# Softmax sums by halves of the queries instead of odd and even key steps, in an attention kernel with a feed-forward layer

## The chip, the cores and the metric

The kernel runs on one core of one Trainium2 chip. The metric is the device time of one execution in microseconds (us). The kernel before takes 433.28 us, the median of six runs from 433.18 to 434.18.

## What is computed

Eight batches, twelve heads, 448 positions, head size 64. Queries and keys are normalised by their root mean square and scaled by a gain, then softmax attention, then a feed-forward layer with a leaky ReLU over the 12 x 64 = 768 features of each of the 3584 positions:

```python
def _attn_ref(q, k, v, g_q, g_k):
    q_n, k_n = (rmsnorm(q, g_q), rmsnorm(k, g_k))
    scores = scale * np.matmul(q_n, k_n.transpose(0, 1, 3, 2))
    scores = scores - np.max(scores, axis=-1, keepdims=True)
    attn = np.exp(scores)
    attn = attn / (np.sum(attn, axis=-1, keepdims=True) + 1e-09)
    return np.matmul(attn, v).astype(np.float32)
...
    h = x @ w_in                       # 3584x768 by 768x2048
    g = np.maximum(0.01 * h, h)
    return (g @ w_out).astype(np.float32)   # 2048x768
```

The division by the sum of the exponentials is what the change touches.

## The kernel before

**Units.** Four heads of one batch are a unit; there are 24, three to a batch. The four heads are numbered by r and a (0 or 1 each). A unit's 448 keys are worked in seven key steps of 64; with r on the two halves of the partitions a step is a tile of 128 rows (2 x 64 keys), and a picks one of two column blocks of 448 queries. The scores stand transposed, keys on partitions and queries in columns, so that the exponentials `et` (128 x 7 steps x 2 x 448, fp16) are at once the moving operand of the product with V.

**Order.** Everything is issued in an order written out by hand (`manual_schedule`). From unit 3 on, a loop goes through units u and four stages d of each. Stage 0 makes the score step 0 of unit u (`qk`, L182), its column maximum on VectorE (`shift_max`, L219 and the diagonal `dg`, L221), the product with V of unit u - 1 (`pv_slot`, L326), the sums of u - 1 (`zcol`, L269), the matmul that spreads the maximum of u (`shift_mm`, L231), from which VectorE takes the shift `eb` (L232, L240), a copy of the product to SBUF on ScalarE (`pv_out`, L281), the addition of the two half sums on VectorE (`zcol_sum`, L286 and L287), and then the exponentials of u (`ex`, L201). The first job after that is `zcol_inv`: the reciprocal as Ln and Exp on ScalarE (L291, L292), and DMAs on SyncE's queue (SP) that spread the reciprocals `zs` over the partitions of `rz` (L296). Behind them on that queue stand the loads of q and k for unit u + 4 (L108) and the stores of results. In stage 1 GpSimd (POOL) multiplies the copied product by `rz` into `xt` (`xmul_pool`, L306), for u from 5 to 7 VectorE does that in stage 2. Stage 2 also has the normalisation of unit u + 2: `rinv` on ScalarE (L147, L148), `n` on VectorE (L154) and its transpose by DMA (L166). Stage 3 squares the rows for unit u + 3 on ScalarE (L131).

**Filling.** Between the attention work of each stage `fill` puts items of the feed-forward layer of earlier batches, by their costs: the first matrix in `moe1` (`hps`, L347, and the leaky ReLU `gt`, L341, on ScalarE), the second in `moe2` (`op`, L387) or in `seven`, which needs seven products where the plain form needs eight (`ma`, `mb`, `mc`, `md`, L427) and prepares sums of operands `sa` and adds results to `ost` on VectorE (L408 to L417, L434).

**The sums.** This path is used for units 4 to 22, 19 in all (`narrow`). A weight of 128 x 32 ones and zeros, `onesr`, adds over the 64 keys of each r, so one matmul gives the sums of two heads on 32 partitions. Four such column tiles of TensorE, at partitions 32 x (2y + a) of the bank `zc`, work side by side. Before, y is the parity of the key step: steps 0, 2, 4 go to y = 0, steps 1, 3, 5 to y = 1, each over all 448 queries, and step 6 is split, its first 224 queries to y = 0 and the others to y = 1. The sum of a query is then the sum of the two rows, which is formed by a copy of 64 x 448 and an addition:

```python
        s["zs"] = zpool.tile([64, S], FP32, tag="zs", name="zs")
        nc.vector.tensor_copy(s["zs"], s["zc"][64:128, 0:S])
        nc.vector.tensor_tensor(s["zs"], s["zc"][0:64, 0:S], s["zs"], op=ALU.add)
```

Row 32a + 2i + r of `zs` holds the sums of head (r, a) sixteen times over, and each of the two DMAs reads 32 rows of 1792 bytes, four times each, into all 128 partitions.

Of the kernel before, what the change touches and what calls it, by code (L numbers as in the profile page):

```python
# [8 lines left out]
FP32 = mybir.dt.float32  # L9
FP16 = mybir.dt.float16  # L10
AF = mybir.ActivationFunctionType
ALU = mybir.AluOpType
AXL = mybir.AxisListType
# [5 lines left out]
def kernel(  # L19
# [11 lines left out]
    nc = tc.nc  # L31

    B, H, S, D = q.shape
    QH = 4
    NS = 7
    P = 128
# [13 lines left out]
    zpool = ctx.enter_context(tc.tile_pool(name="zpool", bufs=1))  # L50
# [4 lines left out]
    def aux(shape, dtype, name):  # L55
        return psum.tile(shape, dtype, tag="aux", bufs=4, name=name)
# [5 lines left out]
    onesr = cst.tile([P, 32], FP16)  # L62
# [184 lines left out]
    def zsum(u, t0=0, t1=NS):  # L247
        s = st[u]
        for t in range(t0, t1):
            for r in range(2):  # L250
                for a in range(2):
                    nc.tensor.matmul(s["zt"][r][64 * a:64 * a + 64, 0:S], ones16[64 * r:64 * r + 64],
                                     s["et"][64 * r:64 * r + 64, t, a], start=(t == 0), stop=(t == NS - 1))

    def zsum_slot(u):
# [2 lines left out]
        s["zt"] = [s["zslot"][:, r] for r in range(2)]  # L258
        zsum(u)

    def zcol(u):
        s = st[u]
        s["zc"] = aux([P, 512], FP32, "zc")
        for t in (0, 1, 6, 2, 3, 4, 5):
            for a in range(2):
                halves = ((t % 2, 0, S),) if t < NS - 1 else ((0, 0, S // 2), (1, S // 2, S))
                for y, lo, hi in halves:
                    c = 32 * (2 * y + a)
                    nc.tensor.matmul(s["zc"][c:c + 32, lo:hi], onesr, s["et"][:, t, a, lo:hi],  # L269
                                     start=(t < 2), stop=(t in (4, 5)))  # L270

    def pv_slot(u):
        s = st[u]
# [8 lines left out]

    def zcol_sum(u):
        s = st[u]
        s["zs"] = zpool.tile([64, S], FP32, tag="zs", name="zs")
        nc.vector.tensor_copy(s["zs"], s["zc"][64:128, 0:S])  # L286
        nc.vector.tensor_tensor(s["zs"], s["zc"][0:64, 0:S], s["zs"], op=ALU.add)  # L287

    def zcol_inv(u):
        s = st[u]  # L290
        nc.scalar.activation(s["zs"], s["zs"], AF.Ln)  # L291
        nc.scalar.activation(s["zs"], s["zs"], AF.Exp, bias=0.0, scale=-1.0)  # L292
        s["rz"] = zpool.tile([P, 2, S], FP32, tag="rz", name="rz")
        for r in range(2):
            src = s["zs"][r:64:2, None, :]
            nc.sync.dma_start(s["rz"][:, r], src.broadcast_to([32, 4, S]))  # L296

    def xmul_sb(u):
        xmul_pool(u, nc.vector)
# [276 lines left out]
    with tc.manual_schedule():  # L576
# [171 lines left out]
        for u in range(3, NU):  # L748
            for d in range(4):
                if d > 0 or u > 3:  # L750
                    qk(u, STEPS[d])
                    if d == 0:
                        shift_max(u)
                        if narrow(u - 1):
                            pv_slot(u - 1)
                            zcol(u - 1)
                            shift_mm(u)
                            pv_out(u - 1)
                            zcol_sum(u - 1)
                        else:  # L760
                            zsum_slot(u - 1)
                            pv(u - 1)
                            shift_mm(u)
                            zinv(u - 1)
                    ex(u)
# [5 lines left out]
                if d == 0:  # L771
                    if u == 3:
                        prep_norm(4)
                        gate(4)
                    elif narrow(u - 1):
                        job(zcol_inv, u - 1)
                    else:
                        xmul(u - 1)
                    if u + 4 < NU:
                        job(load, u + 4)  # L780
                    if u + 3 < NU:
                        load_v(u + 3)
                    if u < 6:
                        prep_sqp(u + 3)
# [63 lines left out]
```

The softmax here doesn't subtract the row's maximum and nothing guards it: scores larger than these inputs give would overflow.

## Time and profile before

| What | Value |
|---|---|
| median of six runs | 433.28 us |
| the profiled execution's own time | 433.18 us |
| its span (first to last instruction) | 431.4 us |
| granted TensorE clock, mean | 0.99 |
| DMA traffic | 62.37 MB, 145 GB/s on average |
| first and last reduction of zs (L286) begin at | 78.9 and 369.1 us |
| zc matmuls (L269) | 304: 16 in each of 19 units |
| rz DMAs (L296) | 38, 224 KB each, 2.9 to 3.7 us from issue to landing |

PE is TensorE's matmuls, PEld its weight loads, DVE VectorE, ACT ScalarE, POOL GpSimd, SP the queue of SyncE. A row of a group gives line, engine, operation, output and inputs, count, and times in nanoseconds (least, median, most). In the timeline the first two columns are start and length in us, and the bracket gives how long the engine stood idle before the instruction and what ended that. In the table of waits come total us, number of times, and the longest. Times of single instructions in the text are starts in us from the beginning of the span. The share of busy time of PE is not its share of peak, since matmuls are pipelined.

### The profile page before, as it was taken

Reading aid. Unit: us, or ns where it says so; the run is one execution under the profiler, and the core shown is the slowest. Engines: PE = TensorE matmul, PEld = TensorE weight load, DVE = VectorE, ACT = ScalarE, POOL = GpSimd, SP = SyncE. Lnnn points to the kernel's source line nnn. Section 1 sums busy time; section 2 is a strip of 40 time slices with the busy share of each in tenths; the row PEclk is TensorE's granted clock in tenths of the full one; section 3 lists DMA queues with packets and bytes.
Section 4 is the critical chain, followed back from the end, with each engine's and each line's share of the span. In section 5 each row is a group of like instructions: output and inputs, shape, how many; then the busy total and the mean of one; then the engine's idle time right before and its main releaser. Section 6 shows DMA issues by size and latency. Waiting matters only on the chain.

```text
span 431.4 us, 8844 instructions
## 1 busy us (share of the span) xinstructions
PE 409.5 (95%) x3645; PEld 211.0 (49%) x3645; DVE 273.4 (63%) x434; ACT 306.1 (71%) x466; POOL 86.7 (20%) x77
## 2 busy tenths in 40 slices
PE   7677999999989999999999999999999999999996
PEld 6444444445444544454445544454445544455563
DVE  5898656888568865487369864587359840542162
ACT  4389888757986779966986789966986757643400
POOL 3875323300002102112102102111101101010000
PEclk9699999999999999999999999999999999999999
DMA  7999993789557896568655897478572460212013
GB/s 254 196 241 250 238 251 99 132 176 235 146 100 118 189 206 164 145 125 212 159 100 139 171 207 169 133 139 207 150 109 45 118 142 17 44 38 73 2 44 103
DMA packets 66476, 62.37 MB, mean 145 GB/s; under 512 B 35716, under 2 KB 61572, under 8 KB 66436
## 3 DMA queue, kind: packets, MB, share of 16 engines
q1 hardware_dynamic: 55840, 49.62, 46.7%
q0 software_dynamic: 10272, 11.80, 17.4%
q8 instruction: 28, 0.46, 0.4%
q10 hardware_dynamic: 324, 0.39, 0.3%
q14 instruction: 12, 0.10, 0.1%
HBM read 45.61 MB, written 11.01 MB: 131 GB/s over the span
## 4 chain that ended last, share of the span: by engine, by line
PE 62%; ACT 16%; DVE 13%; issue 4%; DMA 1%; SPq 0%; ACTq 0%; DVEq 0%
PE hps L347 25%; ACT et L201 8%; PE ma L427 7%; PE md L427 6%; PE sT L182 5%; PE sT L326 4%; PE mc L427 4%; DVE n L154 4%; PE op L387 3%; PE mb L427 3%; ACT gt L341 3%; PE zc L269 2%; DVE sT L219 1%; DVE ssq L142 1%; PE sT L231 1%
## 5 line engine op out<-in xcount | busy, mean ns | idle before, releaser
L201 ACT ACTIVATE et<-sT,eb 128x896 f16<-128x896 f32 x166 | 158.3, 1004 | 15.7 <-PE sT L182 13.3
L347 PE MATMUL hps<-xt,win 128*128 128x448 f16 x756 | 151.0, 353 | 0.2 <-DVE xt L335 0.2
L347 PEld LDWEIGHTS <-win 128*128 128x128 f16 x756 | 70.6, 98 | 71.4 <-issue 9.9
L341 ACT ACTIVATE gt<-hps 128x448 f16<-128x448 f32 x126 | 65.6, 540 | 20.2 <-PE hps L347 19.5
L306 POOL TENSOR_TENSOR xt<-x,rz 128x896 f16<-128x896 f32 x16 | 33.4, 2090 | 150.5 <-DMA rz<-zs 49.7
L154 DVE TENSOR_TENSOR n<-rq,rinv 128x896 f16<-128x896 f32 (+2 forms) x25 | 29.0, 1163 | 48.1 <-ACT rinv L148 44.6
L182 PE MATMUL sT<-qkT 64*64 64x448 f16 x664 | 52.7, 367 | 4.8 <-ACT et L201 4.4
L142 DVE TENSOR_REDUCE ssq<-sq 128x14 f32<-128x896 f32 (+2 forms) x49 | 50.1, 1054 | 1.4 <-ACT sq L131 1.4
L427 PEld LDWEIGHTS <-sa 128*128 128x128 f16 x352 | 32.8, 98 | 26.3 <-issue 6.1
L281 ACT COPY x<-sT 128x896 f32<-128x896 f32 x19 | 17.2, 905 | 39.5 <-DVE sT L232 39.5
L111 POOL DMA_DIRECT2D vt<-in_v_dram x24 | 18.2, 758 | 114.6 <-PE sT L326 107.1
L427 PEld LDWEIGHTS <-gt 128*128 128x128 f16 x264 | 25.2, 98 | 20.3 <-issue 4.3
L219 DVE TENSOR_REDUCE sT<-sT 128x1 f32<-128x896 f32 x22 | 24.0, 1091 | 17.4 <-PE sT L182 17.4
L182 PEld LDWEIGHTS <-qkT 64*64 64x64 f16 x672 | 15.8, 104 | 39.0 <-issue 36.0
L387 PE MATMUL op<-wout,gt 128*128 128x384 f16 x192 | 34.1, 327 | 0.0
L427 PE MATMUL ma<-wout,gt 128*128 128x384 f16 x176 | 32.3, 326 | 0.1
L154 DVE TENSOR_TENSOR n<-rk,rinv 128x896 f16<-128x896 f32 (+2 forms) x25 | 28.9, 1156 | 0.0
L326 PE MATMUL sT<-et,vt 64*64 64x448 f16 x532 | 28.5, 349 | 0.3
L408 DVE TENSOR_TENSOR sa<-gt 128x512 f16<-128x512 f16 (+1 forms) x15 | 8.1, 542 | 29.5 <-ACT gt L341 29.5
L326 PEld LDWEIGHTS <-vt 64*64 64x64 f16 x672 | 20.4, 107 | 10.9 <-issue 1.1
L387 PEld LDWEIGHTS <-gt 128*128 128x128 f16 x192 | 17.7, 98 | 14.0 <-issue 3.2
L453 ACT COPY ost<-ma 128x384 f32<-128x384 f32 x11 | 5.3, 478 | 23.6 <-PE ma L427 23.6
(87 smaller groups left out, 444.5 us busy)
## 6 DMA issues: line engine op xcount, KB each, us to landing
rq<-in_q_dram SPq DMA_DIRECT2D x24, 448.0 KB, 4.8
rk<-in_k_dram SPq DMA_DIRECT2D x24, 448.0 KB, 6.0
out_dram<-ost SPq DMA_DIRECT2D x52, 192.0 KB, 3.9
rz<-zs SPq DMA_DIRECT2D x38, 224.0 KB, 3.3
vt<-in_v_dram POOLq DMA_DIRECT2D x24, 224.0 KB, 5.0
win<-in_moe_w_in_dram POOLq DMA_DIRECT2D x8, 384.0 KB, 9.1
wout<-in_moe_w_out_dram POOLq DMA_DIRECT2D x2, 1536.0 KB, 23.6
out_dram<-ost SPq DMA_DIRECT2D x4, 96.0 KB, 2.1
```

The costliest lines, as they stand in the source:

```text
L111: nc.gpsimd.dma_start(vts[u % NV].rearrange("p a t d -> p a (t d)"), rows(v, u))
L142: nc.vector.tensor_reduce(buf(u, "ssq")[:, ti, :, c[0]:c[1]], buf(u, f"sq{ti}")[:, :, c[0]:c[1]], axis=AXL.X, op=ALU.add)
L154: nc.vector.tensor_tensor(buf(u, "n16")[:, ti, c[0]:c[1]].rearrange("p s a d -> p a s d"), src[:, :, c[0]:c[1]], buf(u, "rinv")[:, ti, :, ...
L182: nc.tensor.matmul(banks[a][64 * r:64 * r + 64, 0:S].rearrange("p (t x) -> p t x", t=NS), kT(u, r, a, t), qT(u, r, a), start=True, stop=True)
L201: nc.scalar.activation(s["et"][:, t], sT[:, :, 0:S], AF.Exp, bias=s["eb"], scale=1.0)
L219: nc.vector.tensor_reduce(s["spare"][:, 511:512], sT[:, :, 0:S], axis=AXL.XY, op=ALU.max)
L306: eng.tensor_tensor(xts[b][:, g], s["x32"], s["rz"], op=ALU.mult)
L326: nc.tensor.matmul(s["pv"][r][64 * a:64 * a + 64, 0:S], vts[u % NV][64 * r:64 * r + 64, a, t], s["et"][64 * r:64 * r + 64, t, a], start=(t ...
L341: nc.scalar.activation(dst, src, AF.Prelu, bias=0.0, scale=1.0, alpha=0.01)
L347: nc.tensor.matmul(hps[:, 0:S], win16[:, kt // 2, kt % 2, ts(ft, P)], xt[:, kt // 2, kt % 2], start=(kt == 0), stop=(kt == KT - 1))
L387: nc.tensor.matmul(op2[:, 0:HC], gt[:, ft, ds(col(t), P)], wout16[:, ft, ds(HC * half, HC)], start=(ft == 0), stop=(ft == FT - 1))
L427: nc.tensor.matmul(bank[:, 0:HC], a[:, f], b[:, f], start=(first and f == 0), stop=(f == HF - 1), skip_group_check=not first)
```

## The change

The column tiles y now stand for the halves of the queries, not for the parity of the steps: tile y takes queries 224y to 224y + 223 of all seven steps. One matmul takes two key steps, as two runs of 224 columns side by side in the bank (steps 0 and 1, 2 and 3, 4 and 5), and step 6 alone fills the first 224 columns only. Each of the 128 partitions then has two columns for a query, 224 apart, and one VectorE reduce adds them. `zs` is 128 x 224 in place of 64 x 448, so are Ln and Exp, and four DMAs of half the size spread it, since a head's sums lie on two groups of partitions. The order of the instructions on every engine is otherwise as before.

```diff
+    HS = S // 2
+
     def zcol(u):
         s = st[u]
         s["zc"] = aux([P, 512], FP32, "zc")
-        for t in (0, 1, 6, 2, 3, 4, 5):
-            for a in range(2):
-                halves = ((t % 2, 0, S),) if t < NS - 1 else ((0, 0, S // 2), (1, S // 2, S))
-                for y, lo, hi in halves:
+        for i, (t, n) in enumerate(((0, 2), (NS - 1, 1), (2, 2), (4, 2))):
+            for y in range(2):
+                for a in range(2):
                     c = 32 * (2 * y + a)
-                    nc.tensor.matmul(s["zc"][c:c + 32, lo:hi], onesr, s["et"][:, t, a, lo:hi],
-                                     start=(t < 2), stop=(t in (4, 5)))
+                    nc.tensor.matmul(s["zc"][c:c + 32, 0:n * HS].rearrange("p (k x) -> p k x", k=n), onesr,
+                                     s["et"][:, t:t + n, a, HS * y:HS * y + HS], start=(i == 0), stop=(i == 3))
...
     def zcol_sum(u):
         s = st[u]
-        s["zs"] = zpool.tile([64, S], FP32, tag="zs", name="zs")
-        nc.vector.tensor_copy(s["zs"], s["zc"][64:128, 0:S])
-        nc.vector.tensor_tensor(s["zs"], s["zc"][0:64, 0:S], s["zs"], op=ALU.add)
+        s["zs"] = zpool.tile([P, HS], FP32, tag="zs", name="zs")
+        nc.vector.tensor_reduce(s["zs"], s["zc"][:, 0:S].rearrange("p (k x) -> p x k", k=2), axis=AXL.X, op=ALU.add)
...
     def zcol_inv(u):
...
         for r in range(2):
-            src = s["zs"][r:64:2, None, :]
-            nc.sync.dma_start(s["rz"][:, r], src.broadcast_to([32, 4, S]))
+            for y in range(2):
+                src = s["zs"][64 * y + r:64 * y + 64:2, None, :]
+                nc.sync.dma_start(s["rz"][:, r, HS * y:HS * y + HS], src.broadcast_to([32, 4, HS]))
```

## The prediction

> **What bounds the kernel now.** I read the head of the page and its slices first, then the tables of waits, then the timeline around each wait of TensorE (PE), and last the tiles zs, zc and rz, which the change touches.
>
> ```profile
> span 431.4 us, 8844 instructions
> ...
> PE 409.5 (95%) x3645; PEld 211.0 (49%) x3645; DVE 273.4 (63%) x434; ACT 306.1 (71%) x466; POOL 86.7 (20%) x77
> ...
> PE   7677999999989999999999999999999999999996
> ```
>
> From slice 8 on PE is full. An engine that gets less to do brings nothing by that alone; only what shortens a wait of PE counts. The table of waits has these for PE after the first units:
>
> ```profile
> PE sT L182 <- ACT et L201: 4.4, 11, 0.9
> ...
> PE sT L231 <- DVE dg L221: 2.3, 4, 1.1
> ...
> PE md L427 <- DVE ost L434: 1.3, 4, 0.3
> ```
>
> L231 is the shift's matmul, which waits for the diagonal dg; its four waits stand in the timeline at 91.64 (0.81), 122.34 (1.10), 185.89 (0.17) and 282.51 us (0.22). Of the 4.4 us at L182 only two, 0.26 us each, lie where the change works (83.41 and 96.94); the others lie before 73 us, ahead of the first zc at 77.21. So all that is to be had is about 4.1 us, and part of it hangs on engines that the change does not help.
>
> **What the change costs and saves by itself.** The rows of tile zs:
>
> ```profile
> L296 SPq DMA_DIRECT2D rz<-zs x38: 520/586/649, 81.6 to 372.9; - x38
> L286 DVE COPY zs<-zc x19: 626/627/628, 78.9 to 369.1; 64x448 f32<-64x448 f32 x19
> L287 DVE TENSOR_TENSOR zs<-zc,zs x19: 616/616/619, 79.5 to 369.8; 64x448 f32<-64x448 f32 x19
> L291 ACT ACTIVATE zs<-zs x19: 566/569/571, 80.4 to 371.1; 64x448 f32<-64x448 f32 x19
> L292 ACT ACTIVATE zs<-zs x19: 576/577/577, 81.0 to 371.7; 64x448 f32<-64x448 f32 x19
> ```
>
> *PE.* 16 zc matmuls a unit before and after; each of the four column tiles streams 3 x 448 + 224 columns either way, four tiles at a time, in the same places of PE's order. The 16 take 0.85 us in the timeline. The moving data now come in two runs of 224; the score matmuls (L182) read seven runs of 64 at 367 ns each against 353 ns for hps, which reads one run. I take 0. Upper end: one round of four (0.19 us between starts) lost in each unit, 19 x 0.19 = 3.6 us. Lower end 0, since no column goes away.
>
> *VectorE.* Copy and add, 0.627 + 0.616 = 1.24 us, become one reduce over 448 PSUM elements a partition. The nearest row is L214, a reduce of 128x448 from PSUM at 0.61 us. Saved 0.63 us a unit, 12 us in all. It buys no time: the next VectorE work after zs at 81 and 94.5 us first waits 0.80 us for PE (op L387), and elsewhere VectorE waits 4 to 6 us for rinv a little later. Should the stride of 224 make it twice as slow, it costs the pair's 1.24 us again and hides as the pair does.
>
> *ScalarE.* Ln and Exp go from 448 to 224 elements a partition. Ln: 128x448 takes 0.534 and 128x896 0.917 (L316, L312), 0.19 for 224, so 0.569 becomes 0.38; with the 128x28 row (0.329, L147) it would be 0.44. Exp: 0.576 and 0.950 (L317, L313), so 0.577 becomes 0.39. Saved 0.32 to 0.38; I take **0.35 us a unit**.
>
> *SyncE and the DMAs.* Two rz transfers become four of half the bytes. Each issue takes 0.586 us, so the last one is issued 1.76 us after the first, not 0.59, and all that SP issues behind it (the loads of q and k, output stores) comes 1.17 - 0.35 = 0.8 us later. The loads are four units ahead; the stores' buffers are four deep, and the transposes of the normalised tile, the next SP work with a deadline, begin 0.85 us (87.98), 1.4 us (101.38) and elsewhere over 2.5 us after the end of such a burst. I charge 0; where that cover were gone, 0.8 us a unit of a transpose that is itself read some 5 us later.
>
> **The one price that decides.** POOL multiplies x by rz (L306) when the last rz has landed, and VectorE's normalisation (L154) does not run beside it:
>
> ```profile
> 178.81 2.07 POOL L306 TENSOR_TENSOR xt<-x,rz 128x896 f16<-128x896 f32 x1 [8.06 <-ACT et L201]
> ...
> 180.30 0.23 ACT L148 ACTIVATE rinv<-uu 128x28 f32<-128x28 f32 x1
> ...
> 180.56 1.28 DVE L154 TENSOR_TENSOR n<-rq,rinv 128x896 f16<-128x896 f32 x1 [5.75 <-ACT rinv L148]
> 181.76 1.08 DVE L154 TENSOR_TENSOR n<-rk,rinv 128x896 f16<-128x896 f32 x1
> ...
> 185.89 0.22 PE L231 MATMUL sT<-dg,onesp 128*128 128x64 f16 x2 [0.17 <-DVE dg L221]
> ```
>
> The first n lasts 1.28 us, not 1.08: its work begins only when POOL ends at 180.88. So when rz lands matters. Call d the landing of the last of four pieces, less that of the last of two, both from the first issue. Now the first piece lands 2.9 us after its issue and the second 3.6 to 3.7 after its own, so 4.2 to 4.3 after the first issue; the two landings lie 1.3 us apart though the issues lie 0.59 apart, so the transfers queue. Half the bytes at half the time (0.65) would end at 2.9 - 0.65 + 3 x 0.65 = 4.2 us: d = 0. A lower end: only the issues limit, 1.76 + 2.25 = 4.0, d = -0.2. An upper end: each piece holds the queue as long as a whole one, 2.9 + 3 x 1.3 = 6.8, d = +2.5. I take **d = 0**: the nearest row is this same transfer, and its queue shows that bytes, not the count, set its pace now. Exp ends 0.35 earlier, so POOL's xt moves by -0.35 + d. Behind xt on POOL stands only the next load of v, which waits for PE's pv anyway (107.1 us in all).
>
> The Trainium skill speaks against splitting: "DMA: Bandwidth & Descriptors", Rules for kernel authors, says of two transfers to disjoint halves that one should not bother, they serialize, and that small ones should be coalesced. Its fit (2.0 us plus bytes over 436 GB/s, for the other kind of queue) gives, as an estimate, 2.3 us for a half piece, so 1.76 + 2.3 = 4.1 us and d = -0.1 to -0.2 if the halves don't serialize, and more if they do. "SBUF — State Buffer", Door 1, says that 64 partitions reach only half of the DMA ports, and the same ones for 0..31 and 0..63; by it, the pieces from the upper 64 partitions use the other half of the ports and queue less, d below 0. No row before the change shows such a piece.
>
> **The sum, wait by wait.**
> - 122.34 us, 1.10: ScalarE is busy 12.77 of 13.00 us from 108 to 121, n at 115.53 had waited 4.09 us for rinv, and from there VectorE runs without a break to dg. The multiply there is VectorE's own, so POOL plays no part. Ln and Exp lie ahead of rinv in this run: **-0.35**.
> - 96.94 us, 0.26: the exponentials at 95.00 come behind Exp, their scores are there from about 94.8: **-0.2**. The same at 83.41 is given back at 91.64, where VectorE is busy from 80.97 on and sets the end.
> - 185.89 and 282.51: rinv and POOL's xt both come 0.35 earlier, VectorE's run to dg too, and the 0.17 + 0.22 go: **-0.4**.
> - 91.64 (0.81) and the four at md (0.31 each): set by VectorE's own run and by PE's scores; 0.
>
> Sum -0.95 us against the profiled execution's own 433.18 us (span 431.4, the rest outside it), which is the lowest of the six runs; their median is 433.28, 0.1 above: **432.2 us**. A measurement of this kernel tells about 0.2%, 0.87 us, from no change.
>
> **Rivals.**
> 1. *Hidden anyway, 432.8 (432.4 to 433.6).* Each of the four waits is followed back through a chain in which PE sets other links (the ost copies wait for op, exponentials for scores). If these end next, half of the 0.95 or nothing is left. For it: PE at 95%; against it: ScalarE without a break before 115.5 and 180.6.
> 2. *Late rz: slower.* Place: POOL's xt ahead of n. In four stages n begins 0.2 us after POOL ends, as here, and PE waits for md behind it:
>
> ```profile
> 147.03 2.07 POOL L306 TENSOR_TENSOR xt<-x,rz 128x896 f16<-128x896 f32 x1 [7.49 <-ACT ost L453]
> ...
> 149.33 1.09 DVE L154 TENSOR_TENSOR n<-rq,rinv 128x896 f16<-128x896 f32 x1 [0.31 <-ACT rinv L148]
> ```
>
> These four lose from d = 0.35 + 0.2 = 0.55 on, the two dg stages from d = 0.35. At d = 1.2 xt is 0.85 late: 4 x 0.65 + 2 x 0.85 = 4.3, less the 0.55 of the first two terms: +3.8, 437. At d = 2.5, 2.15 late: 4 x 1.95 + 2 x 2.15 + some 1.5 in each of two further stages with n behind xt (165.92, 213.41) - 0.55 = 14.6, 448. It decides from d = 0.8, where the loss passes 0.87 us. Against it: bytes halve, and the queue is free between the issues.
> 3. *The matmuls do not keep their rate*, up to +3.6 less 0.95: 436. Nothing in the rows speaks for it but that no zc row reads two runs. The change would then not do what it says, the same work in fewer instructions.
>
> **How the numbers follow.** Forecast 0.43, rival 1 0.36, rival 2 0.16, rival 3 0.05. Faster by over 0.2% is the forecast, 0.43; within it 0.36; slower 0.16 + 0.05 = 0.21. The likeliest case alone is 431.6 to 432.4. The range goes from 431.2 (all waits of ScalarE's making gone, and d = -0.2) to 434.6 (d = 0.9 in rival 2); it leaves out some 0.15 above, most of rivals 2 and 3.
>
> **What would show it.** zc: 16 matmuls in 0.85 us again. zs: one reduce at 0.6 us, Ln and Exp at 0.35 to 0.45. rz: the time from the first issue to POOL's xt (now 147.03 - 142.80 = 4.2 us): 4.2 proves d = 0, above 5 rival 2. The waits of L231 near 122 down to 0.75, near 185 and 282 gone. The prediction is wrong if n still starts where it did (rival 1), or if the waits at md grow above 0.31.

## The result and the profile after

The median after is **432.47 us** (431.50 to 433.13, 19 runs), against 433.54 us for the kernel before in the same comparison (432.46 to 434.87, 41 runs): 1.07 us less, a ratio of 0.9975, 95% interval 0.9968 to 0.9981. The profiled span went from 431.4 to 430.4 us. The diff adds one line, so L296 of before is L297 here, L306 is L307, L427 is L428 and L434 is L435.

The head of the page and its engines, after:

```profile
span 430.4 us, 8910 instructions
...
PE 409.0 (95%) x3645; PEld 210.5 (49%) x3645; DVE 261.8 (61%) x415; ACT 300.6 (70%) x466; POOL 86.4 (20%) x77
```

VectorE is busy for 11.6 us less and ScalarE for 5.5 us less, but the span is only 1.0 us shorter. The rows of tile zs, after (line, engine, operation, tiles, count; least, median and most ns; first and last start):

```profile
L297 SPq DMA_DIRECT2D rz<-zs x76: 520/597/1458, 81.2 to 372.8; - x76
L287 DVE TENSOR_REDUCE zs<-zc x19: 614/625/626, 78.7 to 367.9; 128x224 f32<-128x448 f32 x19
L291 ACT ACTIVATE zs<-zs x19: 389/399/401, 80.3 to 369.9; 128x224 f32<-128x224 f32 x19
L292 ACT ACTIVATE zs<-zs x19: 389/389/391, 80.8 to 370.4; 128x224 f32<-128x224 f32 x19
```

The reduce takes what one instruction of the old pair (copy and add) took, Ln and Exp together are 0.36 us shorter, and there are twice as many DMA issues of 0.6 us each, with one of 1.46. What counts is the table of waits, of which these are PE's rows after the first units:

```profile
PE sT L182 <- ACT et L201: 3.8, 9, 0.9
...
PE sT L231 <- DVE dg L221: 1.8, 2, 1.0
...
PE md L428 <- DVE ost L435: 1.3, 4, 0.3
```

L231 stands 0.5 us lower and on 2 waits, not 4; md is where it was. L182 stands 0.6 us lower and on 9 waits, not 11, but most of that row lies ahead of the first zc and differs from profile to profile. Only two of its waits lie behind it, at 83 and 97 us; they went from 0.26 to 0.10 us each, and waits that short are not listed. In the timeline these are the waits of L231 that are left, with the place at 184.85 that had 0.17 before and now has none:

```profile
91.58 0.22 PE L231 MATMUL sT<-dg,onesp 128*128 128x64 f16 x2 [0.97 <-DVE dg L221]
...
121.84 0.22 PE L231 MATMUL sT<-dg,onesp 128*128 128x64 f16 x2 [0.81 <-DVE dg L221]
...
184.85 0.23 PE L231 MATMUL sT<-dg,onesp 128*128 128x64 f16 x2
```

The start of a profile scatters: in nine of the ten profiles of this study nothing ahead of the first zc matmul differs, and yet it begins anywhere between 76.6 and 77.5 us. So I count from the first zc matmul to the end of the span: 354.19 us before, 353.21 after, **0.98 us less**. The gaps of PE longer than 0.1 us in that stretch, added up from the trace, fell from 4.18 to 3.27 us, which is 0.91 less; all gaps together, the shorter ones too, fell from 4.53 to 3.72, which is 0.81 less. So most of the time came out of PE's waits.

### The profile page after: what moved, and what is told of

Same layout as the page of the kernel before. It is cut to its first block, busy times and chain, and to the rows that moved or that the text cites. A ratio compares the mean times of both kernels' runs of the same rounds, so it can differ in the third digit from the quotient of the medians.

```text
span 430.4 us, 8910 instructions
## 1 busy us (share of the span) xinstructions
PE 409.0 (95%) x3645; PEld 210.5 (49%) x3645; DVE 261.8 (61%) x415; ACT 300.6 (70%) x466; POOL 86.4 (20%) x77
## 4 chain that ended last, share of the span: by engine, by line
PE 71%; ACT 11%; DVE 9%; issue 2%; DMA 1%; SPq 1%; DVEq 0%; ACTq 0%
PE hps L348 30%; ACT et L201 7%; PE ma L428 7%; PE sT L182 6%; PE md L428 6%; PE op L388 5%; PE sT L327 4%; PE mc L428 4%; PE mb L428 3%; DVE n L154 3%; PE zc L270 3%; ACT gt L342 1%; DVE sT L219 1%; PE sT L231 1%; DMA out_dram<-ost 1%
## 5 line engine op out<-in xcount | busy, mean ns | idle before, releaser
L307 POOL TENSOR_TENSOR xt<-x,rz 128x896 f16<-128x896 f32 x16 | 33.5, 2093 | 146.8 <-DMA rz<-zs 123.7
L154 DVE TENSOR_TENSOR n<-rq,rinv 128x896 f16<-128x896 f32 (+2 forms) x25 | 31.2, 1250 | 49.7 <-ACT rinv L148 46.2
L182 PE MATMUL sT<-qkT 64*64 64x448 f16 x664 | 52.7, 367 | 4.7 <-ACT et L201 3.8
L428 PEld LDWEIGHTS <-sa 128*128 128x128 f16 x352 | 32.8, 98 | 26.3 <-issue 6.1
L428 PEld LDWEIGHTS <-gt 128*128 128x128 f16 x264 | 25.2, 98 | 20.3 <-issue 4.3
L182 PEld LDWEIGHTS <-qkT 64*64 64x64 f16 x672 | 15.5, 104 | 38.6 <-issue 35.8
L428 PE MATMUL ma<-wout,gt 128*128 128x384 f16 x176 | 32.3, 326 | 0.0
L154 DVE TENSOR_TENSOR n<-rk,rinv 128x896 f16<-128x896 f32 (+2 forms) x25 | 26.1, 1044 | 0.0
## 6 DMA issues: line engine op xcount, KB each, us to landing
win<-in_moe_w_in_dram POOLq DMA_DIRECT2D x8, 384.0 KB, 11.6
```

The source lines that it names most:

```text
L154: nc.vector.tensor_tensor(buf(u, "n16")[:, ti, c[0]:c[1]].rearrange("p s a d -> p a s d"), src[:, :, c[0]:c[1]], buf(u, "rinv")[:, ti, :, ...
L182: nc.tensor.matmul(banks[a][64 * r:64 * r + 64, 0:S].rearrange("p (t x) -> p t x", t=NS), kT(u, r, a, t), qT(u, r, a), start=True, stop=True)
L307: eng.tensor_tensor(xts[b][:, g], s["x32"], s["rz"], op=ALU.mult)
L428: nc.tensor.matmul(bank[:, 0:HC], a[:, f], b[:, f], start=(first and f == 0), stop=(f == HF - 1), skip_group_check=not first)
```

## The experiments

The theory to be tested: a full PE gains only where one of its waits ends earlier, and here ScalarE's 0.36 us per unit, ahead of rinv and of the exponentials, is the one saving that reaches such waits; the four DMAs cost about what the two did. The rivals: VectorE's saved 0.62 us did it; or the four pieces did cost time (late rz), and the gain is what was left over.

**One part alone: ScalarE.** The kernel before, with Ln and Exp on half of the columns; the reciprocals of the other half are left out.

```diff
-        nc.scalar.activation(s["zs"], s["zs"], AF.Ln)
-        nc.scalar.activation(s["zs"], s["zs"], AF.Exp, bias=0.0, scale=-1.0)
+        half = s["zs"][:, 0:S // 2]
+        nc.scalar.activation(half, half, AF.Ln)
+        nc.scalar.activation(half, half, AF.Exp, bias=0.0, scale=-1.0)
```

> The kernel before, with ScalarE's part of the change alone: Ln and Exp run over the first 224 of the 448 columns of zs only, everything else as before (copy and add on VectorE, two rz DMAs). It leaves out the reciprocal of half of the queries' sums. Theory (the gain comes from ScalarE, through rinv and the exponentials, at the waits of L231 near 122, 185 and 282 us): the whole gain and a little more, since rz lands 0.35 us earlier too: ratio to before 0.9975, 432.5 us against 433.5; the wait of L231 near 122 falls from 1.1 to about 0.8, those near 185 and 282 go. Rival (the gain comes from VectorE's saved instruction): no change, ratio 1.000. Rival (the gain comes from the four smaller DMAs): no change.

Measured 431.84 us, ratio 0.9965 (0.9952 to 0.9978); 1.29 us less than before from the first zc on. Its rows of Ln and Exp, and what is left at L231:

```profile
L292 ACT ACTIVATE zs<-zs x19: 379/382/384, 79.9 to 369.3; 64x224 f32<-64x224 f32 x19
L293 ACT ACTIVATE zs<-zs x19: 389/390/392, 80.3 to 369.7; 64x224 f32<-64x224 f32 x19
```

```profile
PE sT L231 <- DVE dg L221: 1.8, 2, 1.0
```

```profile
91.15 0.22 PE L231 MATMUL sT<-dg,onesp 128*128 128x64 f16 x2 [0.98 <-DVE dg L221]
...
121.41 0.22 PE L231 MATMUL sT<-dg,onesp 128*128 128x64 f16 x2 [0.81 <-DVE dg L221]
```

These are the same two waits as after the whole change, and those near 185 and 282 are gone. The shorter instructions of ScalarE alone give all of the gain. They seem to give some more, but the two ratios' intervals overlap.

**One part alone: VectorE.** The kernel before, without the add (the sums of half of the key steps are left out).

```diff
-        nc.vector.tensor_copy(s["zs"], s["zc"][64:128, 0:S])
-        nc.vector.tensor_tensor(s["zs"], s["zc"][0:64, 0:S], s["zs"], op=ALU.add)
+        nc.vector.tensor_copy(s["zs"], s["zc"][0:64, 0:S])
```

> The kernel before, with VectorE's part of the change alone: the addition of the two half sums is left out, so one copy of 64 x 448 (0.63 us) stands where copy and add took 1.24 us. It leaves out the sums of the odd key steps. Theory (ScalarE): no change, ratio 1.000 (433.5 us); VectorE only waits 0.6 us longer for PE (op) at 81 and 94.5 us and for the transposes elsewhere. Rival (VectorE's saving is the gain): ratio 0.9975, 432.5 us, with the wait of L231 near 91.6 falling too.

Measured 433.43 us, ratio 0.9997 (0.9984 to 1.0011); 0.06 us more than before from the first zc on. Its table of waits has four waits at L231 again, within 0.05 us of what they were before (and at L182 11 waits again):

```profile
PE sT L231 <- DVE dg L221: 2.3, 4, 1.1
```

0.6 us off VectorE in each of 19 units, 12 us in all, buys nothing that can be measured. That rival falls.

**The four pieces alone.** The kernel after, with VectorE's and ScalarE's old amount of work: the reduce runs twice, Ln and Exp on 448 columns, and the four DMAs read the first half.

```diff
-        s["zs"] = zpool.tile([P, HS], FP32, tag="zs", name="zs")
-        nc.vector.tensor_reduce(s["zs"], s["zc"][:, 0:S].rearrange("p (k x) -> p x k", k=2), axis=AXL.X, op=ALU.add)
+        s["zs"] = zpool.tile([P, S], FP32, tag="zs", name="zs")
+        for h in range(2):
+            nc.vector.tensor_reduce(s["zs"][:, HS * h:HS * h + HS], s["zc"][:, 0:S].rearrange("p (k x) -> p x k", k=2),
+                                    axis=AXL.X, op=ALU.add)
...
-                src = s["zs"][64 * y + r:64 * y + 64:2, None, :]
+                src = s["zs"][64 * y + r:64 * y + 64:2, None, 0:HS]
```

> The changed kernel without either saving: the reduce runs twice, into the two halves of a 128 x 448 tile (1.24 us on VectorE, as copy and add took), and Ln and Exp run over its 448 columns (0.57 us each, as before); layout of the matmuls and the four DMAs as in the changed kernel. The second half is computed and not used. Theory (ScalarE): the gain goes, and POOL's xt comes later by the 0.1 to 0.3 us that four DMAs take longer than two: ratio to before 1.000 to 1.001 (433.5 to 434.0), with L231's waits near 185 and 282 at 0.3 to 0.5. Rival (the DMAs or the matmuls' layout make the gain): 432.5 us.

Measured 434.02 us, ratio 1.0016 (1.0001 to 1.0030); 0.48 us more than before from the first zc on. Its waits:

```profile
PE sT L182 <- ACT et L201: 5.1, 11, 1.2
...
PE sT L231 <- DVE dg L221: 2.0, 2, 1.2
```

The size came as expected, the place did not: the waits at 185 and 282 us are not longer but shorter, 0.11 and 0.12 us, and I do not know why. The wait behind a copy of VectorE at 131.7 us is 0.16 where it was 0.11 before, and the one near 122 is 1.16, not 1.10. All gaps of PE behind the first zc together are 4.60 us, 0.07 more than before, and 0.13 us more lies behind the last matmul, so most of the 0.48 does not lie in waits (and the larger sum at L182 comes from waits ahead of the first zc). So the four pieces cost something of this order, at the edge of what can be told, but which link pays was not found. The three parts add up to -1.7 - 0.1 + 0.5 = -1.3 us by the medians and to -1.29 + 0.06 + 0.48 = -0.75 us from the first zc on; the whole change measured -1.07 and -0.98.

**Late rz on purpose.** The kernel after, with each piece cut in two, eight DMAs of 56 KB per unit.

```diff
-                src = s["zs"][64 * y + r:64 * y + 64:2, None, :]
-                nc.sync.dma_start(s["rz"][:, r, HS * y:HS * y + HS], src.broadcast_to([32, 4, HS]))
+                for h in range(2):
+                    c = HS // 2 * h
+                    src = s["zs"][64 * y + r:64 * y + 64:2, None, c:c + HS // 2]
+                    nc.sync.dma_start(s["rz"][:, r, HS * y + c:HS * y + c + HS // 2], src.broadcast_to([32, 4, HS // 2]))
```

> The changed kernel with each rz DMA cut in two (112 columns each, eight issues in place of four). The last issue comes 7 x 0.64 = 4.5 us after the first and not 1.9, so POOL's xt comes 2.6 us later. Theory (a late xt holds up VectorE's n, and n the waits at md and L231; the price of the prediction's second rival): four stages with md lose about 2.6 - 0.34 = 2.25 each, the two stages of L231 about 2.4 each, two further stages about 1.5 each: some 13 to 17 us more than the changed kernel, 446 to 450 us. Rival (the lateness is hidden by fillers): under 2 us more, 432.5 to 434.5.

Measured 448.09 us, ratio 1.0361 (1.0317 to 1.0406); 15.3 us more than after from the first zc on. Its waits of PE:

```profile
PE sT L231 <- DVE dg L221: 8.9, 9, 1.6
PE md L430 <- DVE ost L437: 8.4, 4, 2.2
```

And its timeline around one of the four md stages:

```profile
150.79 2.08 POOL L309 TENSOR_TENSOR xt<-x,rz 128x896 f16<-128x896 f32 x1 [10.41 <-ACT uu L147]
150.98 2.84 DVE L154 TENSOR_TENSOR n<-rq,rinv 128x896 f16<-128x896 f32 x1 [0.31 <-ACT rinv L148]
...
154.75 0.54 DVE L437 TENSOR_TENSOR ost<-md,ost 128x384 f32<-128x384 f32 x1
155.34 1.46 PE L430 MATMUL md<-tw,gt 128*128 128x384 f16 x8 [2.06 <-DVE ost L437]
```

POOL begins 0.19 us before n, and n lasts 2.84 us instead of 1.09: it ends 0.95 us after POOL does (152.87), little less than its own length later. Then the rest of VectorE's queue is late, and PE waits 2.06 us where it waited 0.31. The bracket of xt names uu, which was long done; the last rz lands at 150.53, and that is what xt waited for. This is the prediction's rival 2, with its link and the expected total. The split is not as expected: the four md waits grew by 7.1 us (9.0 expected), and L231 waits in nine places for 7.1 us more in all, where 7.8 were expected from four stages. Late rz is dear here, and the change stayed just short of it.

**The other half of the waits.** What still held PE after the change? At 91.58 and 121.84 us VectorE is busy without a break up to dg, and in each of these runs lies a job that forms half of a difference of w_out (`weight_sum`, into `tw`, 0.95 us). In the kernel after, the one at 88.79 is moved to a later stage and the one at 118.83 to an earlier one:

```diff
-                if d in (1, 3) and 4 <= u < 8:
-                    job(weight_sum, u - 4, d // 2)
+                if d == 1 and 4 <= u < 8:
+                    job(weight_sum, u - 4, 0)
+                if (u, d) in ((4, 3), (6, 3), (7, 1)):
+                    job(weight_sum, u - 4, 1)
+                if (u, d) == (6, 0):
+                    job(weight_sum, 1, 1)
```

> The changed kernel with two halves of the differences of w_out (tw, 0.95 us each on VectorE) taken out of VectorE's run ahead of dg: the one at 88.8 us goes to the next unit's first stage, the one at 118.8 to the second stage of the same unit, where VectorE waits 3.8 us for rinv. Theory (the waits of L231 near 91.6, 0.97 us, and 122, 0.81 us, are set by VectorE's own run to dg): both go, 1.3 to 1.7 us less than the changed kernel, some 431 us, less up to 0.5 where the moved half now stands in the way of xt near 102. Rival (these waits are set by rinv or by PE): no change, 432.5 us.

Measured 430.85 us, ratio 0.9939 (0.9926 to 0.9951) against before, 1.53 us less than after from the first zc on. Of the waits that this study treats, its table lists only the four at md:

```profile
PE md L428 <- DVE ost L435: 1.3, 4, 0.3
```

At L231 the longest is 0.11 us, at 90.81.

The same move in the kernel before tells whether the change is still worth its price once VectorE's run is short:

> The kernel before with the same two halves of tw moved. Theory: 1.4 to 1.8 us less than before, some 431.9 us. The wait near 122 is then nearly gone without the change under study, so of that change's gain of 1.0 us the 0.3 at 122 should be missing, and the 0.2 at 83, which was given back at 91.6, should appear: the changed kernel with moved halves beats this one by 0.5 to 0.9 us. Rival (ScalarE's gain is spread over all units): still by 1.0 us or more.

Measured 431.80 us, ratio 0.9957 (0.9944 to 0.9969). Its row at L231:

```profile
PE sT L231 <- DVE dg L221: 0.7, 3, 0.3
```

The change is worth 0.95 us here (431.80 - 430.85), and 1.03 from the first zc on, a little more than expected. The times do not tell this from the rival's 1.0 or more; the waits do. Before with the sums moved still waits 0.26 and 0.27 at L182 (83 and 96 us), 0.24 at 121, 0.19 at 184 and 0.26 at 281, together 1.2 us; with the change on top none of the five is over 0.10. So the gain sits at five places and is not spread over all units. I had held the wait at 121 for VectorE's alone, and the one at 83 was no longer given back, since VectorE's run behind it had become shorter.

**No ScalarE at all.** In the kernel after, one VectorE instruction in place of Ln and Exp:

```diff
-        nc.scalar.activation(s["zs"], s["zs"], AF.Ln)
-        nc.scalar.activation(s["zs"], s["zs"], AF.Exp, bias=0.0, scale=-1.0)
+        nc.vector.reciprocal(s["zs"], s["zs"])
```

> The changed kernel with one VectorE reciprocal on 128 x 224 in place of ScalarE's Ln and Exp. ScalarE saves another 0.78 us a unit. Theory (ScalarE's saving counts only where it ends a wait of PE): the wait near 122 falls by its remaining 0.8 us at most, nothing else is left for ScalarE to shorten; VectorE's reciprocal, of which no row tells the length, stands in VectorE's run: at 0.5 us it hides in the 1.6 us that VectorE waits for op, and the gain is about 0.7 us (431.8); at 2 us it delays the run to dg at 91.6 and rz by over 1 us, and the kernel is slower by 2 us or more. Rival (each microsecond of ScalarE counts in every unit): 0.78 x 19 = up to 15 us less.

Measured 436.71 us, ratio 1.0072 (1.0058 to 1.0086), about 4.2 us above after. The row of the reciprocal, a wait of ScalarE that after does not have, and a stage that loses:

```profile
L291 DVE RECIPROCAL zs<-zs x19: 1553/1553/1554, 79.4 to 373.2; 128x224 f32<-128x224 f32 x19
```

```profile
108.94 0.54 ACT L341 ACTIVATE gt<-hps 128x448 f16<-128x448 f32 x1 [0.39 <-PE hps L347]
```

```profile
146.15 0.55 DVE L443 COPY ost<-ma 128x384 f32<-128x384 f32 x1
146.75 1.46 PE L427 MATMUL ma<-wout,gt 128*128 128x384 f16 x8 [0.50 <-DVE ost L443]
```

Another 0.79 us off ScalarE in each unit brings nothing: the waits at 91 and 121 stay (1.00 and 0.82). At 121 the row of ScalarE says why: ahead of rinv it now waits for PE's hps, so PE sets the next link, and n still waits 3.82 us for rinv. And 1.55 us more on VectorE, which brought nothing when 0.62 was taken away, costs: at four places PE waits 0.50 to 0.63 us for a copy of VectorE, at two 0.76 for sa. The free time of VectorE is real, but it does not stretch to 1.5 us at every point of a unit.

**The last wait.** The kernel with the sums moved, with the waiting jobs of a step let out before the leftover ones at d = 2, so that VectorE adds md before the second normalisation and not after it:

```diff
+        if d == 2:
+            flush()
```

> The kernel with moved halves (of the changed kernel), and in the third stage the pending addition to ost is issued ahead of the second normalisation and not behind it. Theory (the four waits at md, 0.31 us each, come from the addition that stands behind the two n on VectorE): they go, 1.0 to 1.2 us less than with the moved halves alone, some 430 us; the second n and its transpose come up to 0.55 us later in every unit, which no wait of PE shows. Rival: the later n shifts the run to dg, and new waits of L231 take it back.

Measured **429.35 us**, ratio 0.9898 (0.9885 to 0.9912), the fastest of all, 4.35 us under before in its own comparison. Its span and engines, and the only wait of those discussed that its table still lists:

```profile
span 427.4 us, 8910 instructions
...
PE 408.8 (96%) x3645; PEld 210.0 (49%) x3645; DVE 261.0 (61%) x415; ACT 300.8 (70%) x466; POOL 86.7 (20%) x77
```

```profile
PE sT L231 <- DVE dg L221: 0.2, 1, 0.2
```

In its timeline the add of md now stands between the two normalisations, and the next matmuls wait for nothing:

```profile
147.73 1.09 DVE L154 TENSOR_TENSOR n<-rq,rinv 128x896 f16<-128x896 f32 x1 [0.31 <-ACT rinv L148]
148.74 0.55 DVE L435 TENSOR_TENSOR ost<-md,ost 128x384 f32<-128x384 f32 x1
149.21 1.08 DVE L154 TENSOR_TENSOR n<-rk,rinv 128x896 f16<-128x896 f32 x1
149.87 1.46 PE L428 MATMUL md<-tw,gt 128*128 128x384 f16 x8
```

The instructions are the same as in the kernel with the sums moved; two lines of order took another 1.5 us. That is more than the 1.0 to 1.2 expected: the four waits at md were 1.26 us, and the rival's new wait came too, but small (0.25 us at 91.33, 0.11 without the reordering). The rest is not placed.

## Why the prediction was right

Predicted were 432.2 us and -0.95 us; measured are 432.47 us and -1.07 us between the medians, -0.98 us between the profiles from the first zc on. The sum started from a profiled execution of 433.18 us, and the median of before in the comparison is 433.54, so the difference is what to compare. The mechanism, ScalarE's saving at a few waits of PE, is shown. The steps:

- **PE, zc: 0.** Holds. The 16 matmuls take 0.85 us in the timeline as before; two runs of 224 in place of one of 448 cost nothing, and rival 3 falls.
- **VectorE: 0.63 us a unit, worth nothing.** Holds: 0.625 us against the pair's 1.24, which saves 0.62, and the experiment without the add shows that this is worth nothing.
- **ScalarE: 0.35 us a unit.** 0.36 measured, and the experiment on ScalarE alone shows that the gain comes from here.
- **The wait at 122: -0.35.** 1.10 became 0.81, -0.29.
- **The wait at 96.94: -0.2, and 83.41 given back at 91.64.** Both waits at L182 went from 0.26 to 0.10, and 91 from 0.81 to 0.97: -0.16 - 0.16 + 0.16.
- **185.89 and 282.51: -0.4.** Both gone, -0.39.
- **md and 91.64: 0.** md is unchanged at four times 0.31. That VectorE's order and not ScalarE sets them is shown by the last experiment for md, and by the moved sums for 91.64.
- **The pieces, d = 0.** In the stages where POOL multiplies, its xt came 4.2 to 4.45 us after the first issue before the change and comes 4.3 to 4.54 after it; the pairs give d between -0.07 and +0.32, some +0.1 as a rule. (One stage, near 206 us, had 5.24 and has 5.25.) So d is near 0, but not for the reason given, that the bytes of the pieces queue. Each piece lands about 2.3 us after its own issue, and the four issues are 1.9 us apart from first to last (predicted 1.76): 1.9 + 2.3 = 4.2 us. The issues set the pace, which was the prediction's lower end. One stage is off: there the four issues take 3.17 us, since the second takes 1.27 instead of 0.6, and d is +0.6. After:

```profile
141.64 2.52 SPq L297 DMA_DIRECT2D rz<-zs  x4
146.14 2.08 POOL L307 TENSOR_TENSOR xt<-x,rz 128x896 f16<-128x896 f32 x1 [7.38 <-DMA rz<-zs]
...
221.99 3.17 SPq L297 DMA_DIRECT2D rz<-zs  x4
...
227.04 2.06 POOL L307 TENSOR_TENSOR xt<-x,rz 128x896 f16<-128x896 f32 x1 [8.36 <-DMA rz<-zs]
...
227.26 2.13 DVE L415 TENSOR_TENSOR sa<-gt 128x512 f16<-128x512 f16 x1
```

4.50 us in the first stage, 5.05 in the second; there VectorE's sa, an instruction of two inputs in SBUF, starts 0.22 us behind POOL and lasts 2.13 us, until 0.29 us after POOL's end, and L231 waits 0.14 us at 235. This wait is new and was not predicted. Its chain is read off the timeline; why the second issue takes so long there is open.

The terms that the timeline shows add up to -0.29 - 0.16 - 0.39 + 0.14 = -0.70, and with a wait of 0.11 us near 132 that is gone, and that the prediction did not list, to the 0.81 that all gaps of PE lost. The other 0.17 of the 0.98 does not lie in gaps and is not placed. Rival 1 (hidden anyway) falls with the waits themselves: those at 97, 122, 186 and 282 became shorter. Rival 2 was real and near: four stages lose from d = 0.55 on, the typical d is 0.1, and one stage reached 0.6.

That the number came so close is in part luck, because two errors offset each other. ScalarE's part alone, with two pieces, gave more than the 0.95 of the sum: 1.29 us from the first zc on, 1.70 by the medians. The four pieces, which the sum has at 0, took some of it back: the whole change is 0.32 us behind ScalarE's part alone from the first zc on and 0.63 by the medians, and the four pieces by themselves measured +0.48. Of the 0.32, the 0.14 at 235 is placed, and 0.13 lies behind the last matmul.

Two sums of rival 2 do not follow from its own terms (four stages from d = 0.55, two from 0.35, less 0.55). The loss passes 0.87 us at d = 0.72, not 0.8, and d = 0.9 gives 435.2 us; the upper bound of 434.6 belongs to d = 0.8. The result lies far from that end.

On the rules: "DMA: Bandwidth & Descriptors" (Rules for kernel authors) says not to bother with two transfers to disjoint partition halves, since they serialize, and the prediction read it as speaking against the change. On this queue nothing is gained by the split, as the page has it: four pieces arrive 0.1 us later than two. That they serialize does not show, since each lands 2.3 us after its own issue. The page's fit gave an estimate of 2.3 us for a half piece alone, and the median from issue to landing is 2.3 us:

```profile
rz<-zs SPq DMA_DIRECT2D x76, 112.0 KB, 2.3
```

The packets show what offsets the count: a packet of a whole piece is 1792 B and takes about 136 ns in the trace of before, one of a half is 896 B and takes 67 ns after (medians). But more pieces do cost: eight, with 4.5 us from the first issue to the last, made the kernel 15.6 us slower. Whether the upper 64 partitions' own half of the ports ("SBUF — State Buffer", Door 1) helped the four pieces is not shown; no run sent four pieces from the lower partitions alone.

## What to carry to other kernels

On an engine that is full, list its waits, follow each back through its chain, and count a saving only where it lies ahead of one of them: 12 us off VectorE were worth nothing, 7 us off ScalarE (19 times 0.36) were worth 1 to 1.7 us, and reordering a few jobs, with nothing saved, was worth 3 us more. Where taking time from an engine gains nothing, adding time to it can still cost, and an engine's second saving need not pay as the first did: look at each point of its queue anew. Where GpSimd's work keeps VectorE's from running, the time at which GpSimd starts is a price in itself, and a transfer that sets this start should be watched at its latest stage, not at its median.

## What the runs showed of the hardware

- A VectorE reduce that adds two elements 224 apart in PSUM (128x224 from 128x448) takes 0.625 us. The reduce at L214, which reads as many neighbouring elements into one column (128x1 from 128x448), takes 0.61.
- A reciprocal on VectorE of 128x224 takes 1.553 us, twice as long as Ln and Exp together on ScalarE (0.79 us).
- Ln and Exp on 64x224 take 0.38 and 0.39 us, on 128x224 0.40 and 0.39: twice the partitions made 0.02 us of difference at most.
- n and sa are VectorE instructions with two inputs in SBUF. Where one starts while POOL's xt runs, and not in its last 0.15 us, it ends at a fixed time after POOL does: n, 1.09 us long otherwise, 0.94 to 0.95 us after it in all 40 such cases of the ten traces (so it lasts 1.28 us at 180.56 before the change, and 2.84 us at 150.98 with eight pieces); sa of 512 columns, 0.42 us long otherwise, 0.28 to 0.29 us after it in 27 cases (2.13 us at 227.26). An n that starts ahead of POOL keeps its length, and POOL's xt is the longer one: with eight pieces n takes 1.09 us from 169.00, and xt 2.50 us from 169.55 instead of 2.08.
